# Pooled attention into a SiLU layer on one core: a prologue with gated dummies and value sums on TensorE

## The chip, the core and the metric

The kernel runs on one core of a Trainium2 chip. A core has five engines that run their own instruction streams and meet at semaphores: TensorE (PE, matrix products, whose weight loads are listed apart as PEld), VectorE (DVE), ScalarE (ACT, activation functions), GpSimd (POOL, which here mainly issues transfers) and SyncE (SP, transfers). Matrix products write into PSUM, eight banks of 128 partitions by 512 float32 values; the other tiles lie in SBUF. The metric is the time of one execution on the device in microseconds (us).

## What is computed

Attention over keys and values that are averaged in groups of eight tokens, then a layer with a SiLU between two matrix products. There are 8 batches, 8 heads, 576 tokens and 64 dimensions a head; the layer goes from 512 to 2048 and back to 512.

```python
def _attn_ref(q, k, v):                      # q, k, v: (8, 8, 576, 64)
    k_p = k.reshape(B, H, Sp, 8, D).mean(axis=3)          # Sp = 72
    v_p = v.reshape(B, H, Sp, 8, D).mean(axis=3)
    scores = np.matmul(q, k_p.transpose(0, 1, 3, 2)) / np.sqrt(D)
    attn = np.exp(scores - np.max(scores, axis=-1, keepdims=True))
    attn = attn / (np.sum(attn, axis=-1, keepdims=True) + 1e-09)
    return np.matmul(attn, v_p)

def _moe_ref(x, w_in, w_out):                # x: (4608, 512)
    h = x @ w_in                             # w_in: (512, 2048)
    return (h * (1.0 / (1.0 + np.exp(-h)))) @ w_out
```

## The kernel before

The kernel works on nine tiles of 512 tokens. While PE does the two products of tile t, the attention of the next batch is slipped in between its matmuls. For the first batch nothing can be hidden that way: its keys, queries and values must be loaded, pooled and multiplied before the first product can start. That stretch, some 20 us, is the prologue, and the change lies there.

The keys and values of a batch are 576 rows (8 heads by 72 groups) of 512 float32 values, eight tokens of 64 each. They are loaded as five "slots" of at most 128 rows, in two tiles: slots 0 to 2, and slots 3 and 4. `slot_sums` adds the eight tokens on DVE, in three halving steps:

```python
    def slot_sums(name, j, halves=False):
        raw = row_tiles[name][j]                       # j = 0: slots 0-2, j = 1: slots 3-4
        dst = rows5[name][:, SA:] if j else rows5[name][:, :SA]
        w = RE // 4 if halves else RE // 2             # RE = 512
        while w > D:                                   # D = 64
            nc.vector.tensor_add(out=raw[..., :w], in0=raw[..., :w], in1=raw[..., w : 2 * w])
            w //= 2
        nc.vector.tensor_add(out=dst, in0=raw[..., :D], in1=raw[..., D : 2 * D])
```

`select_k` and `select_v` bring the sums into the order that the attention needs, with matmuls against an identity matrix (`ident`) or its shifted columns (`shifts`); `copy_k` and `copy_v` take the results out of PSUM. `scores` multiplies keys with transposed queries and takes exponentials on ACT; `denominators` and `numerators` finish the softmax, and the numerators are multiplied into `xT`, the input of the first product:

```python
    def q_transpose(b, a, f):                          # a: heads 0-3 or 4-7, f: half of the tokens
        nc.vector.transpose(out=st["qT"][:, a, ...], in_=st["q_bf"][:, a, ...])

    def scores(b, segs):
        sc = [ps_tile([128, 512], FP32, "at", "sc_ps")[:SP, :w] for s in range(4)]
        for g, i0, i1, cs in seg_cols(segs):
            for c in range(2):
                for s in range(4):
                    nc.tensor.matmul(sc[s][:, cs], lhsT=kz..., rhs=st["qT"]..., start=(c == 0), stop=(c == 1))
        es = ...
        for s in range(4):
            nc.scalar.activation(es[:, s, :], sc[s], func=AF.Exp, scale=score_scale)

    def numerators(b, segs, tags=("at", "at")):        # (cut)
        for c in range(2):
            nu_ps = ps_tile([128, 512], FP32, tags[c], "nu_ps")
            ...                                        # four matmuls each, from vp and es
        for c in range(2):
            nc.vector.tensor_mul(out=xT[...], in0=nu[c]..., in1=rec...)
```

PSUM tiles come from two rings of banks, `banks = dict(mm=3, at=5)`: a new tile takes the bank of the one three (or five) before it and waits until that one has been read. `part(g, f)` is heads 4g to 4g+3 with half f of the tokens, written (g, f) in this text. The prologue itself:

```python
    def warm_up(n):                                    # dummies: keep TensorE's clock up
        for _ in range(n):
            nc.tensor.matmul(warm_ps, lhsT=warm[:, :128], rhs=warm, start=True, stop=True)

    ...                                                # loads of keys, queries, values
    nc.gpsimd.memset(shifts, 0.0)
    make_identity(nc, ident, nomemset=True)
    ...
    warm_up(19)
    slot_sums("k", 0)
    select_k(0, 0)
    copy_k(0, 0, act_copy)
    warm_up(4)
    q_transpose(0, 0, 0)
    scores(0, part(0, 0))
    slot_sums("k", 1)
    warm_up(3)
    select_k(0, 1)
    copy_k(0, 1, act_copy)
    q_transpose(0, 1, 0)
    warm_up(2)
    scores(0, part(1, 0))
    denominators(0, part(0, 0))
    slot_sums("v", 0)
    warm_up(2)
    select_v(0, 0, "mm")
    copy_v(0, 0, act_copy)
    denominators(0, part(1, 0))
    q_transpose(0, 0, 1)
    scores(0, part(0, 1))
    slot_sums("v", 1)
    warm_up(1)
    numerators(0, part(0, 0), ("mm", "at"))
    warm_up(2)
    select_v(0, 1, "mm")
    copy_v(0, 1)
    q_transpose(0, 1, 1)
    warm_up(2)
    numerators(0, part(1, 0), ("mm", "at"))
    scores(0, part(1, 1))
    warm_up(2)
```

Each line puts its instructions at the end of its engine's stream; every engine goes through its stream in order. After this the first product of tile 0 starts: for the first `GA` of 16 groups of hidden columns it does the first 288 tokens (`hp_ps`, then SiLU on ACT), then their other 224, and the rest of the groups with all 512 at once. The denominators and numerators of the second token halves, (0, 1) and (1, 1), are slipped in between.

Of the kernel before, what the change touches and what calls it, by code (L numbers as in the profile page):

```python
# [27 lines left out]
FP32 = mybir.dt.float32  # L28
# [8 lines left out]
def kernel(  # L37
# [9 lines left out]
    nc = tc.nc  # L47

    B, H, S, D = q.shape
    POOL = 8  # L50
    SP = S // POOL
# [30 lines left out]
    singles = ctx.enter_context(tc.tile_pool(name="singles", bufs=1))  # L82
# [8 lines left out]
    def ps_tile(shape, dtype, tag, name):  # L91
        return psum.tile(shape, dtype, tag=tag, bufs=banks[tag], name=name)
# [2 lines left out]

    shifts = singles.tile([128, SP + 128 + SP], BF16, name="shifts")
    ident = shifts[:, SP : SP + 128]
    ones = singles.tile([SP, 32], BF16, name="ones")
    warm = singles.tile([128, 512], BF16, name="warm")
    w_in_sb = singles.tile([128, KF, d_ff], BF16, name="w_in_sb")  # L100
# [49 lines left out]
    def q_transpose(b, a, f):  # L150
        st = batches[b]
        n = QF * D
        nc.vector.transpose(  # L153
            out=st["qT"][:, a, f * QF : (f + 1) * QF].rearrange("r i c p -> r (i c p)"),
            in_=st["q_bf"][:, a, f * n : (f + 1) * n],
        )
# [60 lines left out]
    def k_transpose(b, parts=(0, 1)):  # L217
        st = batches[b]
        kT_ps = ps_tile([128, 2, 2, SP], BF16, "at", "kT_ps")
        for a in parts:  # L220
            for c in range(2):
# [10 lines left out]
    RE = POOL * D  # L232
    ROWS = H * SP
    SLOTS = ROWS // 128
    REST = ROWS - 128 * SLOTS
    k5, v5 = (singles.tile([128, SLOTS + 1, D], BF16, name=f"{n}5") for n in "kv")
    rows5 = {"k": k5, "v": v5}


    SA = SLOTS - 1  # L240
    row_tiles = {
        n: [
            big.tile([128, m, RE], FP32, tag=f"{n}_raw2", name="raw") if i else
            raw_tile(f"{n}_raw", H, full=True)[:, : m * RE].rearrange(
                "r (i e) -> r i e", e=RE
            ) for i, m in enumerate((SA, SLOTS + 1 - SA))
        ] for n in "kv"
    }
# [20 lines left out]
    def slot_sums(name, j, halves=False):  # L269
        raw = row_tiles[name][j]  # L270
        dst = rows5[name][:, SA:] if j else rows5[name][:, :SA]
        w = RE // 4 if halves else RE // 2
        while w > D:
            nc.vector.tensor_add(  # L274
                out=raw[..., :w], in0=raw[..., :w], in1=raw[..., w : 2 * w]
            )
            w //= 2
        nc.vector.tensor_add(out=dst, in0=raw[..., :D], in1=raw[..., D : 2 * D])


    def segments(h):
        r = SP * h
        while r < SP * (h + 1):
            i = r // 128
            e = min(SP * (h + 1), 128 * (i + 1))
            yield i, (128 if i < SLOTS else REST), r - 128 * i, r - SP * h, e - r
            r = e

    def select_k(b, a):
        st = batches[b]  # L290
        if a == 0:
            st["kz_ps"] = ps_tile([128, 2, 2, SP], FP32, "at", "kz_ps")
        for c in range(2):
            for s in range(4):
                for i, n, r, sp, m in segments(4 * a + s):
                    nc.tensor.matmul(  # L296
                        st["kz_ps"][32 * s : 32 * (s + 1), a, c, sp : sp + m],
                        lhsT=k5[:n, i, c * DH : (c + 1) * DH],
                        rhs=ident[:n, r : r + m], start=True, stop=True,
                    )  # L300

    def copy_k(b, a, copy=nc.vector.tensor_copy):
        copy(out=kz[b % 2][:, a], in_=batches[b]["kz_ps"][:, a])
# [15 lines left out]
    def copy_v(b, a, copy=nc.vector.tensor_copy):  # L319
        hs = slice(4 * a, 4 * (a + 1))  # L320
        copy(out=batches[b]["vp"][:, hs, :], in_=batches[b]["v_ps"][:SP, hs, :])
# [3 lines left out]
    def part(g, f):  # L325
        return ((g, f * QF, (f + 1) * QF),)
# [6 lines left out]
    def width(segs):  # L333
        return QP * sum(i1 - i0 for _, i0, i1 in segs)
# [5 lines left out]
            yield g, i0, i1, slice(o, o + n)  # L340
            o += n

    def scores(b, segs):
        st = batches[b]
        w = width(segs)
        sc = [ps_tile([128, 512], FP32, "at", "sc_ps")[:SP, :w] for s in range(4)]
# [3 lines that stand above are left out]
                    rows = slice(32 * s, 32 * (s + 1))  # L350
                    nc.tensor.matmul(  # L351
                        sc[s][:, cs],
                        lhsT=kz[b % 2][rows, g, c, :],
                        rhs=st["qT"][rows, g, i0:i1, c, :],
                        start=(c == 0), stop=(c == 1),
                    )
        es = mid.tile([SP, 4, VW], BF16, tag="es", bufs=4, name="es")[:, :, :w]
        for s in range(4):
            nc.scalar.activation(es[:, s, :], sc[s], func=AF.Exp, scale=score_scale)  # L359
        st["es", segs] = es  # L360


    def denominators(b, segs, on_dve=False):
        st = batches[b]
        w = width(segs)
        es = st["es", segs]
        den_ps = ps_tile([128, 512], FP32, "at", "den_ps")
        for s in range(4):
            nc.tensor.matmul(  # L369
                den_ps[32 * s : 32 * (s + 1), :w],  # L370
                lhsT=ones, rhs=es[:, s, :], start=True, stop=True,
            )
        rec = mid.tile([128, VW], FP32, tag="rec", bufs=4, name="rec")[:, :w]
        if on_dve:
            nc.vector.reciprocal(rec, den_ps[:, :w])
        else:
            lnd = mid.tile([128, VW], FP32, tag="lnd", name="lnd")[:, :w]
            nc.scalar.activation(lnd, den_ps[:, :w], func=AF.Ln)  # L378
            nc.scalar.activation(rec, lnd, func=AF.Exp, scale=-1.0)
        st["rec", segs] = rec  # L380
# [318 lines left out]

    warm_ps = ps_tile([128, 512], FP32, "mm", "warm_ps")  # L700

    def warm_up(n):
        for _ in range(n):
            nc.tensor.matmul(warm_ps, lhsT=warm[:, :128], rhs=warm, start=True, stop=True)  # L704

    load_slots(nc.sync, 0, "k", 0, 2)
    load_slots(nc.scalar, 0, "k", 2, 3)
# [8 lines left out]
    attn_tables()  # L716
    nc.vector.memset(warm, 0.0)
    nc.vector.memset(ones, float(POOL))
    nc.gpsimd.memset(shifts, 0.0)
    make_identity(nc, ident, nomemset=True)  # L720

    for n in "kv":
        nc.vector.memset(row_tiles[n][1][REST:, SLOTS - SA], 0.0)
# [12 lines left out]
        load_w_in(512 * c, 512 * (c + 1))  # L736

    act_copy = nc.scalar.copy
    warm_up(19)
    slot_sums("k", 0)  # L740
    select_k(0, 0)
    copy_k(0, 0, act_copy)
    warm_up(4)
    q_transpose(0, 0, 0)
    scores(0, part(0, 0))
    slot_sums("k", 1)
    warm_up(3)
    select_k(0, 1)
    copy_k(0, 1, act_copy)
    q_transpose(0, 1, 0)  # L750
    warm_up(2)
    scores(0, part(1, 0))
    denominators(0, part(0, 0))
    slot_sums("v", 0)
    warm_up(2)
    select_v(0, 0, "mm")
    copy_v(0, 0, act_copy)
    denominators(0, part(1, 0))
    q_transpose(0, 0, 1)
    scores(0, part(0, 1))  # L760
    slot_sums("v", 1)
    warm_up(1)
    numerators(0, part(0, 0), ("mm", "at"))
    warm_up(2)
    select_v(0, 1, "mm")
    copy_v(0, 1)
    q_transpose(0, 1, 1)
    warm_up(2)
    numerators(0, part(1, 0), ("mm", "at"))
    scores(0, part(1, 1))  # L770
    warm_up(2)
    load_slots(nc.gpsimd, 1, "k", 0, 3)
    load_slots(nc.gpsimd, 1, "k", 3, 4)
    load_slots(nc.gpsimd, 1, "k", 4, 5)
# [14 lines left out]
    for t in range(NT):  # L789
        a = t + 1  # L790
        f_up, f_down = [], []
        if t == 0:
            GA = 11
            items = [(g, 0, HS) for g in range(GA)]
            items += [(g, HS, NTT - HS) for g in range(GA)]
            items += [(g, 0, NTT) for g in range(GA, KG)]
            f_up += [(1, lambda: denominators(0, part(0, 1), on_dve=True))]
            f_up += [(5, lambda: denominators(0, part(1, 1), on_dve=True))]
            f_up += [(13, lambda: numerators(0, part(0, 1)))]
            f_up += [(17, lambda: numerators(0, part(1, 1)))]  # L800
        else:
            G = lambda *gs: [(g, 0, NTT) for g in gs]
            if t == 1:
                items = (
                    G(12, 13, 14, 15) + [(0, "251")] + G(8) + [(0, "43")] + G(9)
                    + [(0, "7h6")] + G(10) + [(0, "s")] + G(11, 0, 1, 2, 3)
                )
            else:
                items = (
                    G(12, 13) + [(0, "251")] + G(14) + [(0, "43")] + G(15) + [(0, "76")]  # L810
                    + [(1, "2")] + [(0, "hs")] + [(1, "51")] + G(0) + [(1, "43")] + G(1)
                    + [(1, "7h6")] + G(2) + [(1, "s")] + G(3)
                )
            for n in U_X:
                f_up.append((0, lambda n=n: unit_x_sum(t, n)))
            for n in (2, 5):
                f_up.append((36 if t > 1 else 45, lambda n=n: hidden_sum(n, 4, 8)))
            f_up.append((56, lambda: hidden_sum(6, 4, 8)))
            for n, k0 in ((2, 0), (5, 0), (1, 4), (1, 0)):
                f_up.append((64, lambda n=n, k0=k0: hidden_sum(n, k0, k0 + 4)))  # L820
            f_down.append((33, lambda: hidden_sum(7, 0, 8)))
            f_down.append((71, lambda: hidden_sum(6, 0, 4)))
# [99 lines left out]
```

The softmax here doesn't subtract the row's maximum and nothing guards it: scores larger than these inputs give would overflow.

## Time and profile before

| what | value |
|---|---|
| time, median of 3 runs | 287.23 us (286.76 to 287.54) |
| span of the profiled execution | 284.8 us |
| granted TensorE clock | 1.000 |
| PE busy | 278.0 us (98%) |
| DVE busy | 225.1 us (79%) |
| ACT busy | 183.8 us (65%) |
| POOL busy | 52.2 us (18%) |
| first dummy matmul | 1.20 us |
| DVE begins the first key sums | 5.28 us |
| DVE begins the sums of the last value slots | 13.48 us |
| first SiLU | 20.04 us |

A profile is one execution as the hardware's profiler recorded it. A row of the timeline gives start and length in us, engine, line of the kernel, operation, output and inputs with their shapes, the number of instructions merged in it, and in brackets the idle time of the engine before it and what ended that. The chain that ended last is followed back from the last instruction, at each step to what released it. A line such as `L274` is that of the kernel before.

### The profile page before, as it was taken

To read this page: it belongs to the slowest core of one execution; us is meant where nothing else is said; L and a number is where in the kernel's file an instruction comes from. 1 tells how busy PE (TensorE), PEld (TensorE's weight loads), DVE (VectorE), ACT (ScalarE), POOL (GpSimd) and SP (SyncE) were. 2 spreads that over 40 slices of the span, in tenths; PEclk is the share of its full clock that TensorE was granted. 3 is DMA by queue.
4 is the path that set the end of the run, shared out by engine and by line. 5 is a ranking of instruction groups with operands and counts; after the bars stand their busy time and mean duration, and the time that the engine had idled before them with its cause. 6 is when DMAs were issued, how large, how long until landed. Compare 5 with 4: busy or idle time off the path is not lost.

```text
span 284.8 us, 6920 instructions
## 1 busy us (share of the span) xinstructions
PE 278.0 (98%) x2773; PEld 196.0 (69%) x2793; DVE 225.1 (79%) x403; ACT 183.8 (65%) x359; POOL 52.2 (18%) x68
## 2 busy tenths in 40 slices
PE   8989999999999999999999999999999999999995
PEld 3348544465777677767888886677677867787684
DVE  4887854979969796979698969986998686836773
ACT  1577676458656886688568857794779558325700
POOL 8664317402030011101200101054100000000000
PEclk9999999999999999999999999999999999999999
DMA  7999999793849565964895396839970032005004
GB/s 211 277 266 227 219 306 183 214 199 70 153 69 210 124 96 95 145 148 126 140 177 156 72 147 113 176 59 170 150 142 0 2 85 65 2 9 139 1 3 147
DMA packets 35296, 37.70 MB, mean 132 GB/s; under 512 B 9952, under 2 KB 27616, under 8 KB 35264
## 3 DMA queue, kind: packets, MB, share of 16 engines
q0 software_dynamic: 21760, 20.86, 43.0%
q1 hardware_dynamic: 12928, 15.48, 22.2%
q10 hardware_dynamic: 576, 0.92, 0.9%
q8 instruction: 22, 0.36, 0.6%
q14 instruction: 10, 0.08, 0.1%
HBM read 36.70 MB, written 9.44 MB: 162 GB/s over the span
## 4 chain that ended last, share of the span: by engine, by line
PE 94%; DVE 3%; ACT 1%; issue 1%; DVEq 0%
PE hp_ps L547 25%; PE o_psP L655 15%; PE o_psQ L655 15%; PE u_psQ L488 7%; PE u_psP L488 7%; PE o_psR L655 5%; PE sc_ps L351 4%; PE warm_ps L704 4%; PE o_ps L582 3%; PE nu_ps L395 3%; PE u_psR L488 2%; PE den_ps L369 2%; DVE w_sum L633 1%; PE kz_ps L296 1%; DVE xT L404 1%
## 5 line engine op out<-in xcount | busy, mean ns | idle before, releaser
L547 PE MATMUL hp_ps<-xT,w_in_sb 128*128 128x512 bf16 (+3 forms) x397 | 80.8, 338 | 1.4 <-ACT h_T L553 0.4
L655 PEld LDWEIGHTS <-h_sum 128*128 128x128 bf16 x640 | 60.6, 98 | 11.9 <-issue 1.3
L553 ACT ACTIVATE h_T<-hp_ps 128x512 bf16<-128x512 f32 (+2 forms) x95 | 51.4, 546 | 26.3 <-PE hp_ps L547 24.9
L547 PEld LDWEIGHTS <-w_in_sb 128*128 128x128 bf16 x412 | 39.3, 98 | 25.0 <-issue 1.4
L615 DVE TENSOR_TENSOR h_sum<-h_T 128x1024 bf16<-128x1024 bf16 (+1 forms) x72 | 50.8, 743 | 7.0 <-ACT h_T L553 7.0
L359 ACT ACTIVATE es<-sc_ps 72x384 bf16<-72x384 f32 (+1 forms) x100 | 39.0, 470 | 10.0 <-PE sc_ps L351 9.9
L488 PEld LDWEIGHTS <-w_sum 128*128 128x128 bf16 x300 | 29.4, 98 | 7.7
L655 PEld LDWEIGHTS <-h_T 128*128 128x128 bf16 x256 | 24.1, 98 | 4.4 <-issue 0.9
L404 DVE TENSOR_TENSOR xT<-nu_ps,rec 128x384 bf16<-128x384 f32 (+1 forms) x50 | 24.0, 532 | 0.3
L378 ACT ACTIVATE lnd<-den_ps 128x384 f32<-128x384 f32 (+1 forms) x23 | 11.1, 484 | 20.2 <-PE den_ps L369 20.2
L153 DVE STREAM_TRANSPOSE qT<-q_bf 128x576 bf16<-128x576 bf16 x32 | 23.0, 753 | 0.0
L182 POOL DMA_DIRECT2D raw<-in_k_dram x5 | 7.0, 1398 | 79.2 <-DVE h_sum L615 28.8
L496 ACT ACTIVATE h_T<-c_sb 128x512 bf16<-128x512 f32 x30 | 18.1, 625 | 5.0 <-DVE c_sb L520 5.0
L274 DVE TENSOR_TENSOR raw<-raw 128x384 f32<-128x384 f32 (+3 forms) x20 | 12.4, 618 | 7.5 <-DMA raw<-in_v_dram 4.3
L655 PE MATMUL o_psP<-w_out_sb,h_sum 128*128 128x256 bf16 x128 | 17.6, 273 | 0.0
L655 PE MATMUL o_psQ<-w_sum,h_sum 128*128 128x256 bf16 x128 | 16.7, 273 | 0.0
L655 PE MATMUL o_psQ<-w_out_sb,h_sum 128*128 128x256 bf16 x128 | 16.6, 273 | 0.0
L655 PE MATMUL o_psQ<-w_sum,h_T 128*128 128x256 bf16 x128 | 16.5, 273 | 0.0
L655 PE MATMUL o_psP<-w_sum,h_T 128*128 128x256 bf16 x128 | 16.5, 273 | 0.0
L520 DVE TENSOR_TENSOR c_sb<-u_psP,t_sb 128x512 f32<-128x512 f32 x15 | 10.2, 678 | 7.1 <-PE u_psP L488 3.6
L655 PE MATMUL o_psR<-w_sum,h_sum 128*128 128x256 bf16 x128 | 15.7, 273 | 0.0
L655 PE MATMUL o_psP<-w_sum,h_sum 128*128 128x256 bf16 x128 | 15.4, 272 | 0.0
(77 smaller groups left out, 417.1 us busy)
## 6 DMA issues: line engine op xcount, KB each, us to landing
out_dram<-o_sb SPq DMA_DIRECT2D x128, 64.0 KB, 3.0
q_bf<-in_q_dram POOLq DMA_DIRECT2D x6, 576.0 KB, 11.1
raw<-in_k_dram SPq DMA_DIRECT2D x6, 512.0 KB, 5.0
raw<-in_k_dram POOLq DMA_DIRECT2D x5, 576.0 KB, 9.1
raw<-in_v_dram POOLq DMA_DIRECT2D x5, 576.0 KB, 8.6
raw<-in_v_dram SPq DMA_DIRECT2D x5, 512.0 KB, 7.6
w_in_sb<-in_moe_w_in_dram POOLq DMA_DIRECT2D x8, 256.0 KB, 8.4
w_out_sb<-in_moe_w_out_dram POOLq DMA_DIRECT2D x4, 512.0 KB, 13.5
```

The costliest lines, as they stand in the source:

```text
L153: nc.vector.transpose(out=st["qT"][:, a, f * QF : (f + 1) * QF].rearrange("r i c p -> r (i c p)"), in_=st["q_bf"][:, a, f * n : (f + 1) * n],)
L274: nc.vector.tensor_add(out=raw[..., :w], in0=raw[..., :w], in1=raw[..., w : 2 * w])
L351: nc.tensor.matmul(sc[s][:, cs], lhsT=kz[b % 2][rows, g, c, :], rhs=st["qT"][rows, g, i0:i1, c, :], start=(c == 0), stop=(c == 1),)
L359: nc.scalar.activation(es[:, s, :], sc[s], func=AF.Exp, scale=score_scale)
L404: nc.vector.tensor_mul(out=xT[:, 2 * g0 + c : 2 * (g0 + ng - 1) + c + 1 : 2, cols], in0=nu[c][:, :w].rearrange("r (g n) -> r g n", g=ng), ...
L488: nc.tensor.matmul(ps[bank][:, u, :], lhsT=w[:, kk, 128 * u : 128 * (u + 1)], rhs=x[:, kk, :], start=first and u == 0 and kk == 0, stop=kk ...
L496: nc.scalar.activation(h_T[:, g : g + 2, j * NQ : (j + 1) * NQ], src, func=AF.Silu)
L547: nc.tensor.matmul(hp_ps[:, r0:r1], lhsT=w_in_sb[:, kk, g * 128 : (g + 1) * 128], rhs=xT[:, kk, x0 : x0 + r1 - r0], start=(kk == 0), stop= ...
L553: nc.scalar.activation(h_T[:, g, n0 : n0 + n], hp_ps[:, :n], func=AF.Silu)
L615: nc.vector.tensor_tensor(out=h_sum[n][:, ks, :], in0=quarter(*a, ks), in1=quarter(*b, ks), op=op)
L655: nc.tensor.matmul(ps[b][:, c, :], lhsT=left(n, kt, c), rhs=W_OUT[n][:, kt, :], start=b not in begun, stop=kt == k1 - 1, skip_group_check= ...
L704: nc.tensor.matmul(warm_ps, lhsT=warm[:, :128], rhs=warm, start=True, stop=True)
```

## The change

It has four parts.

Only nine dummies run freely at the start. Eight more, in float32 with 128 columns and zero weights, read the last columns of a loaded key slot, so they start once that slot is there. Those columns (384 to 511) are read by the sums but never written by them, so dummies and sums can run side by side.

The last two value slots are no longer summed on DVE: eight float32 matmuls with an identity matrix, one for each of the eight tokens of a group, add up in PSUM (`pool_slots`), and one copy on DVE (`copy_pooled`) rounds the sums to bfloat16. This needs the identity in float32 (`ident32`), from which ACT copies the bfloat16 one. Both value copies are now on DVE.

The two late query transpositions stand together, ahead of that copy; the second key half is summed and selected between the third and fourth exponential of the first scores; the numerators of (0, 0) come after the second value selection; some dummies go.

And `GA` is 12 for 11.

It is meant to take work off DVE in the stretch after the values have landed, and to let the dummies end when the key sums are there.

```diff
@@ -95,6 +95,8 @@
 
     shifts = singles.tile([128, SP + 128 + SP], BF16, name="shifts")
     ident = shifts[:, SP : SP + 128]
+    ident32 = singles.tile([128, 128], FP32, name="ident32")
+    warm32 = singles.tile([128, 128], FP32, name="warm32")
     ones = singles.tile([SP, 32], BF16, name="ones")
     warm = singles.tile([128, 512], BF16, name="warm")
     w_in_sb = singles.tile([128, KF, d_ff], BF16, name="w_in_sb")
@@ -277,6 +279,21 @@
             w //= 2
         nc.vector.tensor_add(out=dst, in0=raw[..., :D], in1=raw[..., D : 2 * D])
 
+
+    def pool_slots(name, p0, p1):
+        if p0 == 0:
+            pooled[name] = ps_tile([128, SLOTS + 1 - SA, D], FP32, "mm", "p_ps")
+        for p in range(p0, p1):
+            nc.tensor.matmul(
+                pooled[name], lhsT=ident32,
+                rhs=row_tiles[name][1][:, :, p * D : (p + 1) * D],
+                start=(p == 0), stop=(p == POOL - 1),
+            )
+
+    def copy_pooled(name):
+        nc.vector.tensor_copy(out=rows5[name][:, SA:], in_=pooled[name])
+
+    pooled = {}
 
     def segments(h):
         r = SP * h
@@ -340,7 +357,7 @@
             yield g, i0, i1, slice(o, o + n)
             o += n
 
-    def scores(b, segs):
+    def scores(b, segs, between=None):
         st = batches[b]
         w = width(segs)
         sc = [ps_tile([128, 512], FP32, "at", "sc_ps")[:SP, :w] for s in range(4)]
@@ -356,6 +373,8 @@
                     )
         es = mid.tile([SP, 4, VW], BF16, tag="es", bufs=4, name="es")[:, :, :w]
         for s in range(4):
+            if s == 3 and between:
+                between()
             nc.scalar.activation(es[:, s, :], sc[s], func=AF.Exp, scale=score_scale)
         st["es", segs] = es
 
@@ -699,9 +718,15 @@
 
     warm_ps = ps_tile([128, 512], FP32, "mm", "warm_ps")
 
-    def warm_up(n):
+    def warm_up(n, ps=warm_ps):
         for _ in range(n):
-            nc.tensor.matmul(warm_ps, lhsT=warm[:, :128], rhs=warm, start=True, stop=True)
+            nc.tensor.matmul(ps, lhsT=warm[:, :128], rhs=warm, start=True, stop=True)
+
+    def warm_behind(rhs, n):
+        for _ in range(n):
+            nc.tensor.matmul(
+                warm_ps[:, : rhs.shape[-1]], lhsT=warm32, rhs=rhs, start=True, stop=True
+            )
 
     load_slots(nc.sync, 0, "k", 0, 2)
     load_slots(nc.scalar, 0, "k", 2, 3)
@@ -716,8 +741,11 @@
     attn_tables()
     nc.vector.memset(warm, 0.0)
     nc.vector.memset(ones, float(POOL))
-    nc.gpsimd.memset(shifts, 0.0)
-    make_identity(nc, ident, nomemset=True)
+    nc.vector.memset(warm32, 0.0)
+    nc.vector.memset(ident32, 0.0)
+    nc.vector.memset(shifts[:, :SP], 0.0)
+    nc.vector.memset(shifts[:, SP + 128 :], 0.0)
+    make_identity(nc, ident32, nomemset=True)
 
     for n in "kv":
         nc.vector.memset(row_tiles[n][1][REST:, SLOTS - SA], 0.0)
@@ -736,39 +764,44 @@
         load_w_in(512 * c, 512 * (c + 1))
 
     act_copy = nc.scalar.copy
-    warm_up(19)
+    act_copy(ident, ident32)
+    warm_up(9)
+    warm_behind(row_tiles["k"][0][:, SA - 1, RE - 128 :], 8)
     slot_sums("k", 0)
     select_k(0, 0)
     copy_k(0, 0, act_copy)
     warm_up(4)
     q_transpose(0, 0, 0)
-    scores(0, part(0, 0))
-    slot_sums("k", 1)
-    warm_up(3)
-    select_k(0, 1)
-    copy_k(0, 1, act_copy)
+
+    def rest_k():
+        slot_sums("k", 1)
+        warm_up(3)
+        select_k(0, 1)
+        copy_k(0, 1, act_copy)
+
+    scores(0, part(0, 0), rest_k)
     q_transpose(0, 1, 0)
     warm_up(2)
     scores(0, part(1, 0))
     denominators(0, part(0, 0))
     slot_sums("v", 0)
-    warm_up(2)
+    pool_slots("v", 0, 3)
     select_v(0, 0, "mm")
-    copy_v(0, 0, act_copy)
+    pool_slots("v", 3, 5)
     denominators(0, part(1, 0))
+    pool_slots("v", 5, POOL)
     q_transpose(0, 0, 1)
+    q_transpose(0, 1, 1)
+    copy_pooled("v")
+    copy_v(0, 0)
     scores(0, part(0, 1))
-    slot_sums("v", 1)
     warm_up(1)
-    numerators(0, part(0, 0), ("mm", "at"))
-    warm_up(2)
     select_v(0, 1, "mm")
     copy_v(0, 1)
-    q_transpose(0, 1, 1)
-    warm_up(2)
+    numerators(0, part(0, 0), ("mm", "at"))
     numerators(0, part(1, 0), ("mm", "at"))
     scores(0, part(1, 1))
-    warm_up(2)
+    warm_up(2, ps_tile([128, 512], FP32, "mm", "warm_ps"))
     load_slots(nc.gpsimd, 1, "k", 0, 3)
     load_slots(nc.gpsimd, 1, "k", 3, 4)
     load_slots(nc.gpsimd, 1, "k", 4, 5)
@@ -790,7 +823,7 @@
         a = t + 1
         f_up, f_down = [], []
         if t == 0:
-            GA = 11
+            GA = 12
             items = [(g, 0, HS) for g in range(GA)]
             items += [(g, HS, NTT - HS) for g in range(GA)]
             items += [(g, 0, NTT) for g in range(GA, KG)]
```

## The prediction, made before the changed kernel had run

> **What bounds the kernel now.** I read the page's engine table first: TensorE (PE) is busy 98% of the 284.8 us span and the clock is granted in full, so time is only to be had where PE runs dummies or waits. Next the busy time by stretches, to find where that is.
>
> ```profile
> 8.00:13.48 5.48, 5.31 (x68) 2.33 (x69) 4.46 (x9) 3.46 (x12) 3.01 (x6) 1.00 1.14 280
> 13.48:17.57 4.09, 3.62 (x44) 1.49 (x46) 3.90 (x9) 2.77 (x9) 3.15 (x5) 1.00 1.24 207
> 17.57:20.50 2.93, 2.53 (x22) 1.31 (x21) 2.07 (x3) 2.90 (x7) 1.64 (x3) 1.00 1.18 287
> 20.50:28.40 7.90, 7.90 (x89) 6.07 (x88) 6.24 (x11) 6.13 (x17) 3.38 (x6) 1.00 1.14 248
> ```
>
> The columns after the length are PE, weight loads, DVE, ACT, POOL. From 20.5 us on PE has no idle time at all (7.90 of 7.90), and the stretches to 200 us are as full; before 20.5 much of its work is dummies. So the prologue is worth exactly what it moves the moment at which PE becomes full. In 13.48 to 17.57 DVE is the full one (3.90 of 4.09), in 17.57 to 20.50 ACT is (2.90 of 2.93). Third, the chain that ended last, for that moment:
>
> ```profile
> 15.80 0.42 DVE vp L321
> 16.23 0.69 DVE qT L153
> 16.92 0.04 issue
> 16.96 0.48 PE sc_ps L351 x8
> 17.44 1.29 ACT es L359 x4
> 18.73 0.02 issue
> 18.75 1.28 ACT L414
> 20.03 0.01 issue
> 20.04 0.42 ACT h_T L553
> 20.46 0.04 issue
> 20.50 0.40 PE hp_ps L547 x2
> ```
>
> The last query transposition on DVE releases the last scores, four exponentials and the load of the SiLU table follow on ACT, and the first SiLU at 20.04 frees the bank for which PE waits (PE may run three hp_ps groups ahead, three banks being there). I call that first SiLU S; S = 20.04. Fourth, DVE in order of time, for why the transposition comes so late:
>
> ```profile
> 12.09 0.77 DVE L153 STREAM_TRANSPOSE qT<-q_bf 128x576 bf16<-128x576 bf16 x1
> 13.48 1.15 DVE L274 TENSOR_TENSOR raw<-raw 128x512 f32<-128x512 f32 x2 [0.61 <-DMA raw<-in_v_dram]
> 14.66 0.29 DVE L278 TENSOR_TENSOR v<-raw 128x128 bf16<-128x128 f32 x1
> 14.87 0.81 DVE L404 TENSOR_TENSOR xT<-nu_ps,rec 128x288 bf16<-128x288 f32 x2
> 15.80 0.42 DVE L321 CAST vp<-v_ps 72x256 bf16<-72x256 f32 x1
> 16.15 0.76 DVE L153 STREAM_TRANSPOSE qT<-q_bf 128x576 bf16<-128x576 bf16 x1
> 16.84 0.78 DVE L404 TENSOR_TENSOR xT<-nu_ps,rec 128x288 bf16<-128x288 f32 x2
> ```
>
> DVE idles 0.61 us until the last value slots land at 13.48, then works without a gap to 17.62. Everything early is slack against that landing; what follows it sets S.
>
> [...] The kernel before has no float32 matmul, so no trace here shows it. [...] the dummies' weight loads are 0.43 us apart from 2.02 to 6.3 us, then six take 1.25 us, 0.21 each. [...] The trace shows no matmul overtaking another, and my argument rests on it: a matmul that waits for a DMA holds up all that stand behind it.
>
> **The change part by part.**
>
> *Gated dummies.* Now 19 dummies run from 1.20 to 8.04 while the first key sums end at 7.23: select_k starts about 0.7 us late. After: 9 x 0.43 from 1.20 end at 5.05, and 8 float32 ones start when a key slot has landed (5.28 or a little before). [...] About two at half clock and six at full: 2 x 0.43 + 6 x 0.26 = 2.4, end at 7.7. Gain at select_k 0.3 us. Sums of the second key tile end at 9.27 on DVE whatever PE does, so the second score group is ready perhaps 0.8 us earlier (its copy also moves ahead of the fourth exponential). None of this passes the landing at 13.48: worth 0.0 at S.
>
> *Identity.* Built in float32 on POOL after DVE memsets, and copied by ACT. POOL's affine select ended at 6.39, behind its own 0.38 us memset; the copy should end by about 6.5, before 7.2. Worth 0. POOL issues weights some 0.4 us sooner, but behind the values in its queue, so I keep the landing at 13.45.
>
> *Query transposition (1, f1)* goes from 16.15 into DVE's idle time before the landing (12.86 to 13.63). Takes 0.76 us off DVE after the landing.
>
> *Value sums on PE.* DVE loses 1.15 + 0.29 = 1.44 us and gains a copy of 128x128 from PSUM, about 0.28 (the 72x256 cast takes 0.42). PE gains eight float32 matmuls, c each. The first waits for both late value slots and stands in PE's order before select_v(0), the denominators of (1,0) and the scores of (0,1), which ran from 12.2 to 13.9 beside the transfer. They now run behind the landing.
>
> The chain after the landing, with T1 the end of the last pooling matmul: select_v 0.20 and denominators 0.35 (their steps in the chain of before) make T1 = 13.45 + 0.55 + 8c. Then on PE scores (0,1) 0.45 and a dummy 0.21. On DVE the pooled copy ends at T1 + 0.5 and the first value copy at T1 + 0.9; select_v(1) runs on PE to about T1 + 1.0, and its copy ends at T1 + 1.45. The first two multiplications, 0.81, end at T1 + 2.25. The scores of (1,1) need that: there are five "at" banks, and their fourth tile falls on the bank of the numerators (0,0), which DVE frees there (in PE's order after the change one of these score matmuls has exactly this DVE wait). First finished score tile at T1 + 2.65 as ACT sees it, exponentials 1.30, table load 1.28: S = T1 + 5.25 = 19.25 + 8c.
>
> With c = 0.213[...] S = 20.95, 0.9 later than 20.04. With c = 0.26, my choice, S = 21.33, 1.3 later. With c = 0.43[...] S = 22.7, 2.65 later. The break-even is c = 0.10[...].
>
> *Dummies removed.* Seven of 0.21 us in the middle; they lay in PE's waits. Worth 0.
>
> *GA 11 to 12.* One more hidden group split: four matmuls of 512 columns become four of 288 (55 take 6.14 us, 0.112 each) and four of 224 (about 0.10). 4 x (0.112 + 0.10 - 0.21) = about 0.01, at most 0.1 us on PE. On ACT 0.41 + 0.37 for 0.60.
>
> Sum: +1.3 + 0.05 = +1.35 us at full carry, since PE has no idle time behind S to absorb it. I take +1.2, 288.4 us, the small cut being for the rival below.
>
> **Rivals.** (a) The design works: DVE was the full engine after the landing, it loses 1.44 + 0.76 us there and gains 0.28, so S comes about 1 us earlier, 286.3. For it: DVE's 3.90 of 4.09, and a late transposition on the chain. Against it: PE takes over the sums serially with the blocked work, and all four multiplications plus two copies now stand behind the landing (before, one copy was ACT's and 0.81 us of multiplication filled a wait). This would also come out if the late slots landed a microsecond earlier than 13.4[...]: 0.1 or 0.2 us of this may appear through POOL's shorter work.
> (b) Float32 matmuls expose their weight loads: c near 0.43, eight gated dummies end after 8.5, pooling takes 3.4 us, and the result is +2.7, 289.9. For it: the sizes are small, 128 columns against 128 weight columns, and bf16 loads take 98 ns[...]. Against: eight dummies were evidently meant to cover 5.28 to 7.23, 0.24 each.
> (c) PE cools: it would idle from about 12 to 13.45 waiting for values; if the clock halves there, the next 3 us run at half speed, +0.5 to +1. Against: one gap of 1.5 us, with work on both sides.
> (d) Nothing moves: ACT or the hidden groups reabsorb it, 287.2. Against: PE is full from 20.5 on.
>
> **Range and chances.** Middle 288.4; (b) or (c) reach 289.8, (a) at a third of its strength reaches 286.8. I give (a) about one in five. Range 286.8 to 289.8. Two per cent is 5.7 us, more than the whole part of the prologue that could move: faster 0.005, within 0.985, slower 0.01.
>
> **What would show it.** Right: pooling matmuls start within 0.2 us of 13.45 after a PE wait on the value DMA, spaced 0.21 to 0.30; the first SiLU at 21.0 to 21.8; PE full from there; the first key selection near 7.5 with no effect later. In the last multiplications of the prologue, DVE ends near 19.2 against 17.62. Wrong: first SiLU before 20.0, a landing of the value slots before 12.7, a PE that reaches the pooling after the landing, or idle time of PE between 21 and 45 us that changes against before.

## The result, and the profile after

The changed kernel takes 288.69 us (median of six executions, 288.36 to 289.6) where the kernel before takes 286.97 us (median of six, the three behind the 287.23 us of the start among them): ratio 1.0066, 95% interval 1.0045 to 1.0087. It is slower by 1.7 us; 288.4 us was predicted. The size came out nearly as forecast, but two of the steps behind it did not hold.

The same four stretches in the changed kernel, with the columns PE, weight loads, DVE, ACT, POOL, then granted clock, DMA share and GB/s:

```profile
8.00:13.48 5.48, 3.89 (x42) 1.79 (x41) 5.04 (x9) 3.66 (x12) 3.63 (x6) 0.95 1.14 274
13.48:17.57 4.09, 4.08 (x34) 3.24 (x34) 0.35 (x2) 0.85 (x2) 2.72 (x5) 0.65 1.24 206
17.57:20.50 2.93, 2.40 (x33) 1.14 (x35) 2.15 (x6) 1.84 (x6) 1.47 (x2) 1.00 1.18 295
20.50:28.40 7.90, 7.58 (x74) 4.75 (x72) 7.25 (x10) 6.25 (x15) 3.62 (x6) 1.00 1.14 248
```

Between 13.48 and 17.57 PE and DVE have changed places: DVE falls from 3.90 us to 0.35, PE is full. In the stretch ahead of it PE is busy 3.89 us where it was 5.31. And the clock column has two numbers that no row of the kernel before had, 0.95 and 0.65.

The chain that ended last in the changed kernel, through the prologue (start, length, what):

```profile
4.83 7.98 DMA raw<-in_v_dram
12.81 0.14 issue
12.95 1.62 PE p_ps L287 x6
14.57 0.35 PE v_ps L331 x6
14.92 1.01 PE p_ps L287 x4
15.93 0.36 PE den_ps L388 x3
16.29 0.91 PE p_ps L287 x6
...
18.76 0.81 DVE xT L423 x2
19.57 0.04 issue
19.61 0.36 PE sc_ps L368 x5
19.97 1.28 ACT es L378 x4
21.25 0.02 issue
21.27 1.28 ACT L433
22.56 0.01 issue
22.57 0.42 ACT h_T L572
```

The transfer of the value slots now leads straight into the pooling products (p_ps; each float32 product is recorded as two matmuls, so x6 is three products), with select_v and the denominators between them as forecast, and the chain goes on through the multiplication into xT to the last scores, the exponentials and the table load. The first SiLU, S, is at 22.57 against 20.04. DVE in order of time shows how little is left there:

```profile
11.74 1.43 DVE L155 STREAM_TRANSPOSE qT<-q_bf 128x576 bf16<-128x576 bf16 x2
17.22 0.29 DVE L294 CAST v<-p_ps 128x128 bf16<-128x128 f32 x1 [4.05 <-PE p_ps L287]
```

The two transpositions are done before the landing, as meant; then DVE stands still for 4.05 us until the last pooling product. PE, DVE and ACT each keep to the order of their streams here. PE starts the value selection, whose sums DVE had ready at 11.83, at 14.57, behind three products. DVE takes out its result, which PE finished at 14.92, at 17.43, behind the cast that waited. And ACT starts the fourth exponential of the first scores, which PE finished at 9.05, at 10.58, behind the copy of the second key selection, for which ACT waited 0.33 us.

This profile is one of the two executions out of six (289.6 and 289.3 us) whose mean clock was 0.994 and 0.993; the other four, at 1.000, lie between 288.36 and 288.86 us. To see the change without that, both kernels were profiled again (below, with the experiments). The chain of the changed kernel in its second profile, at full clock throughout, which I call the undisturbed one:

```profile
12.99 0.91 PE p_ps L287 x6
13.90 0.20 PE v_ps L331 x6
14.11 0.53 PE p_ps L287 x4
14.63 0.24 PE den_ps L388 x4
14.87 0.86 PE p_ps L287 x6
15.73 0.37 PE sc_ps L368 x8
...
19.82 1.28 ACT L433
21.11 0.01 issue
21.12 0.42 ACT h_T L572
```

The same steps from the same landing: the pooling pieces take 0.91 + 0.53 + 0.86 = 2.30 us instead of 1.62 + 1.01 + 0.91 = 3.54, and S is 21.12, not 22.57.

### The profile page after: what moved, and what is told of

The parts are those of the page before. It is cut to its first block, busy times and chain, and to the rows that moved or that the text cites. A ratio compares the mean times of both kernels' runs of the same rounds, so it can differ in the third digit from the quotient of the medians.

```text
span 287.7 us, 6964 instructions
## 1 busy us (share of the span) xinstructions
PE 279.1 (97%) x2794; PEld 200.0 (69%) x2813; DVE 224.4 (78%) x406; ACT 184.2 (64%) x360; POOL 52.2 (18%) x67
## 4 chain that ended last, share of the span: by engine, by line
PE 88%; DMA 4%; DVE 3%; issue 1%; POOL 1%; ACT 1%; SPq 0%; DVEq 0%; POOLq 0%
PE hp_ps L566 24%; PE o_psP L674 15%; PE o_psQ L674 14%; PE u_psQ L507 7%; PE u_psP L507 7%; PE o_psR L674 5%; PE sc_ps L368 4%; PE o_ps L601 3%; DMA raw<-in_v_dram 3%; PE nu_ps L414 2%; PE u_psR L507 2%; PE den_ps L388 2%; PE p_ps L287 1%; DVE xT L423 1%; DVE w_sum L652 1%
## 5 line engine op out<-in xcount | busy, mean ns | idle before, releaser
L601 PE MATMUL o_ps<-w_out_sb,h_T 128*128 128x512 bf16 x61 | 14.5, 380 | 0.3 <-issue 0.3
```

The lines of the kernel that those rows point to most:

```text
L601: nc.tensor.matmul(ps, lhsT=h_T[:, g, m * 128 : (m + 1) * 128], rhs=w_out_sb[:, g, :], start=(g == 0), stop=(g == KG - 1),)
```

## The experiments

After the comparison the theory was: in-order work held up behind the landing, plus eight float32 products, plus in some executions a halved clock that follows PE's idle time. The rivals: that the products alone are at fault, that the clock alone is, or that one of the small parts (the gated dummies, the regrouped hidden columns) costs something. S below is from the profile of each kernel. The ratio is against the kernel before on the same chip; it is the recorded one, which differs a little from the quotient of the two medians.

| run | S, us | median, us | before, us | ratio, 95% interval |
|---|---|---|---|---|
| changed kernel | 22.57 | 288.69 | 286.97 | 1.0066 (1.0045 to 1.0087) |
| e1 gap filled | 21.18 | 288.47 | 286.67 | 1.0057 (1.0037 to 1.0076) |
| e2 pooling later | 20.31 | 287.79 | 286.67 | 1.0037 (1.0024 to 1.0051) |
| e3 sums on DVE | 19.50 | 288.34 | 286.67 | 1.0054 (1.0029 to 1.0079) |
| e8 the same, four dummies more | 19.60 | 286.95 | 287.16 | 0.9995 (0.9982 to 1.0008) |
| e7 GA 11 | 22.62 | 289.39 | 286.67 | 1.0081 (1.0051 to 1.0110) |
| e4 gate alone | 19.38 | 287.21 | 287.16 | 1.0008 (0.9994 to 1.0023) |
| e5 early transposition alone | 19.24 | 286.78 | 287.16 | 0.9988 (0.9976 to 1.0000) |
| e6 and early scores | 18.77 | 286.39 | 287.16 | 0.9970 (0.9956 to 0.9984) |
| e12 e6 with the gate | 18.34 | 285.91 | 286.93 | 0.9971 (0.9956 to 0.9986) |

### Six dummies in PE's gap

The edit, on the changed kernel:

```diff
     slot_sums("v", 0)
+    warm_up(6)
     pool_slots("v", 0, 3)
```

> The changed kernel with six more free dummies (6 x 0.21 us) on PE just before the pooling, where its trace shows PE idle for 1.43 us and the clock at half for the 3.4 us that follow. Theory order (the loss is the work that PE holds back behind the wait for the values[...]; the half clock is an extra that only two of the six timed executions showed): clock 1.00 in every execution, pooling products 0.24 to 0.28 us each instead of 0.44, first SiLU near 21.1 us instead of 22.57, median 288.3 us, none above 288.8. Rival clock (the half clock is the whole loss): 287.0 us.

PE's idle time ahead of the first pooling product falls from 1.43 to 0.26 us:

```profile
13.06 0.91 PE L287 MATMUL p_ps<-raw,ident 128*128 128x128 f32 x6 [0.26 <-DMA raw<-in_v_dram]
```

All seven executions ran at a clock of 0.998 to 1.000. The first SiLU comes at 21.18, and from the landing at 13.06 that is 8.12 us, the same as the 8.13 of the undisturbed profile (12.99 to 21.12; a landing is taken here and below as the start of the first instruction that waited for it); the profile with half the clock has 9.62. So the 1.45 us between the two profiles of the changed kernel are the clock, and a held clock leaves nearly the whole loss standing: ratio 1.0057, with one execution (288.95 us) above the 288.8 that was to be the most. The clock is an addition, not the cause of the main loss.

### The pooling behind the scores

The eight products move behind the first scores of the second half, so that select_v(0), the denominators and those scores can run during the transfer:

```diff
     slot_sums("v", 0)
-    pool_slots("v", 0, 3)
+    warm_up(2)
     select_v(0, 0, "mm")
-    pool_slots("v", 3, 5)
     denominators(0, part(1, 0))
-    pool_slots("v", 5, POOL)
     q_transpose(0, 0, 1)
     q_transpose(0, 1, 1)
-    copy_pooled("v")
     copy_v(0, 0)
     scores(0, part(0, 1))
     warm_up(1)
+    pool_slots("v", 0, POOL)
+    copy_pooled("v")
     select_v(0, 1, "mm")
```

> The changed kernel with all eight pooling products behind the scores of (0,1) in PE's order, and the copy of the first values ahead of the pooled copy on DVE: nothing but the second value selection now waits for the late values. Theory order: the first value selection, the denominators (1,0) and the scores (0,1) run before the landing again, first SiLU 20.2 to 20.6 us, time 287.0 to 287.5 us. Rival products (float32 products are slow by themselves, 0.44 us each even without a drop of the clock): first SiLU 21.5, 288.4 us.

The chain that ended last, in this kernel:

```profile
13.22 0.32 PE warm_ps L723
13.54 1.80 PE p_ps L287 x16
15.34 0.02 issue
15.36 0.30 DVE v L294
```

Ahead of the products stands PE's own work, no longer the transfer, and eight products in one piece take 1.80 us: 0.225 us each. S falls from 21.18 to 20.31 against the first experiment, the ratio from 1.0057 to 1.0037, some 0.6 us. The two ran on the same chip, and by the means of their 7 and 13 executions the difference is 0.58 us, with a 95% interval of about 0.2 to 0.9. That is what the blocked order costs. Of the loss, the other two thirds remain, so the time misses the 287.0 to 287.5 us that the theory gave.

### The last value slots summed on DVE again

The order of PE is that of the second experiment, without the products; the gate, the transpositions, the multiplications and the hidden groups stay as changed. The second edit adds four dummies to the first:

```diff
     copy_v(0, 0)
+    slot_sums("v", 1)                    # in place of all pool_slots and copy_pooled
     scores(0, part(0, 1))
-    warm_up(1)
+    warm_up(5)                           # e8 only
     select_v(0, 1, "mm")
```

> The changed kernel with the last value slots summed on DVE again (no pooling products), everything else kept: gated dummies, both late query transpositions ahead of the sums, numerators (0,0) behind the second value selection. Theory order: first SiLU 19.7 to 20.1, time 286.7 to 287.1 us, that is the time before: the whole loss lies in the pooling on PE. Rival arrangement (the loss lies in the numerators and copies that now stand behind the landing): 287.8 us or more.

> The run with the last value sums on DVE (no pooling products) and four more dummies behind the scores of (0,1), where its trace shows PE idle for 0.89 us and the clock at half from 16.3 to 19.8 us. Theory order, amended by that run (there the dummies left out cost as much as the pooling did): clock 1.00 in all executions, first SiLU 19.4 to 19.7 us, time 286.3 to 286.8 us, that is 0 to 0.5 us under before. Rival arrangement: 287.5 us or more with the clock held too.

The first of the two stays at 1.0054: by its time alone the rival, the arrangement, would have been right. But seven of its eight executions had a clock of 0.986 to 0.994, and the only one at 0.998 took 286.77 us. In its profile S is early, 19.50, and yet the time is close to that of the changed kernel. Its stretches around the loss:

```profile
14.00:15.00 1.00, 0.11 (x4) 0.10 (x2) 0.78 (x3) 1.00 (x4) 1.00 (x3) 1.00 1.24 205
17.00:18.00 1.00, 1.00 (x4) 0.32 (x3) 0.22 (x1) 1.00 (x4) 0.11 (x1) 0.50 1.24 202
19.00:20.00 1.00, 1.00 (x8) 0.32 (x6) 1.00 (x1) 0.90 (x2) 0.45 (x2) 0.50 1.14 350
```

PE stands idle for 0.89 us between 14 and 15, waiting for the sums, and from 16.8 to 20.2 each stretch has half the clock. Four dummies in that wait (e8) leave S where it was, 19.60, hold the clock at 0.998 or more in all 14 executions, and bring the ratio to 0.9995. So the arrangement is not the loss. The step from 1.0054 to 0.9995 is 1.7 us for four dummies of 0.21 us.

With the clock held in both, e2 against e8 is the price of the float32 products alone: 1.0037 against 0.9995, 1.2 us. The two ran on different chips, each beside the kernel before, and with both intervals the difference lies between some 0.7 and 1.7 us; at S it is 0.71.

### When the clock halves

Three profiles have the half clock. Where it began and ended is read from short stretches; below are the busy times of that interval and, above it, of one of equal length before it. Changed kernel, then e7, then e3:

```profile
9.48:12.90 3.42, 2.04 (x28) 0.77 (x26) 3.35 (x6) 2.77 (x10) 2.18 (x4) 1.00 1.16 257
12.90:16.31 3.41, 3.36 (x21) 2.89 (x21) 0.27 (x1) 0.44 (x1) 2.58 (x4) 0.50 1.24 205
```

```profile
10.16:13.58 3.42, 2.29 (x31) 1.30 (x29) 3.00 (x5) 2.74 (x9) 2.51 (x4) 1.00 1.16 257
13.58:16.99 3.41, 3.41 (x23) 2.91 (x21) 0.00 (x0) 0.97 (x3) 2.67 (x5) 0.50 1.25 207
```

```profile
13.39:16.80 3.41, 2.31 (x39) 1.00 (x31) 2.85 (x9) 2.19 (x7) 2.95 (x5) 1.00 1.24 206
16.80:20.21 3.41, 3.41 (x22) 1.17 (x18) 1.81 (x3) 2.99 (x6) 1.45 (x3) 0.50 1.21 262
```

Each time the clock is halved for 3.41 us, though PE is full, and each time PE was busy only 2.04 to 2.31 us (60 to 68%) in the 3.41 us before. The longest single gaps were 1.43, 1.13 and 0.89 us. The length of the gap alone does not order the cases, for the undisturbed profile has a gap of 1.06 us and no halving. There the 3.41 us that hold the gap, 10.20 to 13.62, have PE busy for 2.36 us, or 69%. All other stretches of that length, measured end to end through the prologues, were 84% busy or more, and none of them was followed by half a clock. So the busy share orders the cases, but 68% with a halving and 69% without one lie too close together to name a limit, and what decides it was not shown.

The halvings also began close to multiples of 3.41 us after the clock's rise at the start. When that rise came is an estimate from the gated dummies. Eight take 2.02 us where the clock is up already (e4, and the same in e1) and 2.49 in the changed kernel. At half speed half of the time is lost, so 0.47 us lost are 0.94 us at half speed, and the clock rose near 5.01 + 0.94 = 5.95, twice 3.41 and 0.1 us before 12.90. In e7 the same reckoning (2.82 us) gives 6.6, twice 3.41 us before 13.58 to within 0.15, and in e3 (2.76 us) 6.5, three times 3.41 us before 16.80 to within 0.1. Whether that is more than chance, three profiles do not show.

One such halving is 3.41 x 0.5 / 287.7 = 0.6% of the clock's mean. By this estimate an execution at 0.994 had one and one at 0.988 two; a profile with two was not taken.

### GA back to 11

```diff
-            GA = 12
+            GA = 11
```

> The changed kernel with GA = 11. Theory order: within 0.1 us of the changed kernel, 288.6 us. Rival split (the twelfth split hidden group costs PE small products and ACT one more SiLU on the path): 288.3 us or less.

Inconclusive. Five of the eight executions had a clock of 0.988 to 0.994; the three at full clock (287.76, 288.35, 288.77 us) have a mean 0.25 us below that of the four of the changed kernel (288.36 to 288.86), which so few executions do not resolve. The execution that took longest (292.9 us) is left out of the ratio. A difference of less than half a microsecond stays open.

### The gate alone

The kernel before with nine dummies, eight gated ones and the float32 identity, nothing else (new tiles, helper and memsets cut):

```diff
-    warm_up(19)
+    act_copy(ident, ident32)
+    warm_up(9)
+    warm_behind(row_tiles["k"][0][:, SA - 1, RE - 128 :], 8)
```

> The kernel before with the gated dummies alone (9 free ones, 8 float32 ones behind the key slot, identity built in float32 and copied by ACT; values, transpositions and everything later as before). Theory order: first key selection 0.3 to 0.7 us earlier, first SiLU 19.9 to 20.2 us as before, time within 0.3 us of the kernel before. Rival key landing (the gating itself costs time later): slower by 0.8 us or more. Side question, the wait of DVE for key sums near 143 us that every profile of the changed family shows (0.3 to 1.0 us) and that of the kernel before does not: if it comes with the two added 128x128 float32 tiles it shows here and in the dummies run, and not in the other two.

No difference in time: 1.0008, 0.9994 to 1.0023. Yet its first SiLU is at 19.38, earlier than the 19.9 to 20.2 expected and than 20.04 in the profile of before. How far S of one kernel varies had to be known. As to the side question: the wait for key sums does not come with the added tiles, for it is also in e5 (1.2 us) and e6 (1.4 us), which lack them.

### Both kernels again

> The kernel before, unchanged, looked at once more. Question: DVE waits for key sums between 110 and 150 us in every profile since the first one (0.3 to 1.4 us), also in kernels that lack the added tiles. Theory (the margin of those loads is thin in the kernel before too, and varies from one execution to the next): a wait of 0.3 us or more shows here as well. Rival (the changed prologue brings it by shifting the transfers): none here. The landing of the late values: 12.6 to 13.5 us, first SiLU 6.6 to 6.8 us after it.

> As the look before it, a second one, for the spread: theory and rival the same.

> The changed kernel, unchanged, looked at once more, since its first profile had the clock at half for 3.4 us. With the clock held: pooling products near 0.24 to 0.28 us each, first SiLU 7.9 to 8.2 us after the landing of the values (9.6 with the half clock).

PE in order of time, the first key selection, in the first, second and third profile of before:

```profile
7.97 0.28 PE L296 MATMUL kz_ps<-shifts,k 128*32 128x72 bf16 x12
```

```profile
8.26 0.28 PE L296 MATMUL kz_ps<-shifts,k 128*32 128x72 bf16 x12
```

```profile
7.30 0.28 PE L296 MATMUL kz_ps<-shifts,k 128*32 128x72 bf16 x12 [0.22 <-DVE k L278]
```

S is 20.04, 20.33 and 19.37: 12.07 us after the first key selection in all three, and 12.08 in the gated kernel (7.30, 19.38). From the landing of the last value slots (13.48, 12.80, 12.85) it is 6.56, 7.53 and 6.52, not the 6.6 to 6.8 expected. So in the kernel before S is tied to PE's front, not to the landing. The chain that ended last says the same in the first profile already, in the part ahead of the lines shown with the prediction:

```profile
1.20 6.84 PE warm_ps L704 x19
8.04 0.21 PE kz_ps L296 x8
...
15.38 0.33 PE v_ps L314 x6
```

It goes back through PE's work to the first dummies, and no transfer of values stands in it.

The 19 dummies end sooner or later as the clock rises early or late, and all of PE's work behind them moves along: their weight loads close up at 4.54, 6.29 and 7.09 us in the third, first and second profile, and the selection starts at 7.30, 7.97 and 8.26. In the third it waits 0.22 us for the sums, which end at 7.25, so there a still earlier rise would not have started it before 7.3.

In the changed kernel it is the reverse: S is 8.1 us after the landing at full clock whether the first key selection is at 7.31 (e1) or 7.85 (e11). In that profile the changed kernel took 287.57 us, and three executions of before on the same chip 286.86, 286.19 and 286.66. The wait for key sums that the theory expected in the kernel before as well, 0.3 us or more, was not there: none in the second profile, 0.2 us in the third.

### The early transposition, and the last scores ahead of the numerators

Both on the kernel before. The first edit is only the move of the late transposition; the second also moves the last scores:

```diff
     q_transpose(0, 0, 1)
+    q_transpose(0, 1, 1)
     scores(0, part(0, 1))
     ...
     copy_v(0, 1)
-    q_transpose(0, 1, 1)
-    warm_up(2)                               # e6, e12
-    numerators(0, part(1, 0), ("mm", "at"))  # e6, e12
     scores(0, part(1, 1))
+    numerators(0, part(1, 0), ("mm", "at"))  # e6, e12
```

> The kernel before with the last query transposition alone moved ahead of the last value sums, into DVE's idle time before the landing. Theory order: scores (1,1) 0.4 to 0.5 us earlier, first SiLU 19.5 to 19.7 us, time 0.3 to 0.5 us shorter than before. Rival (the transposition is not what the chain needs): within 0.1 us of before.

> As the early transposition, and the scores of (1,1) ahead of the numerators (1,0) in PE's order, so that the last four exponentials follow the four before them on ACT (all dummies but two kept). Theory order: exponentials (1,1) from 16.3 us, first SiLU 18.8 to 19.1 us, time 0.8 to 1.2 us shorter than before. Rival (the multiplications of (1,0) on DVE at 17.6 to 17.9 us bound the first product as much as ACT does): first SiLU 19.5 or later, 0.3 us.

> The kernel before with two parts together: the gated dummies, and the early transposition with the scores of (1,1) ahead of the numerators (1,0). First key selection near 7.3 us in place of 7.3 to 8.3, first SiLU 18.2 to 18.5 us. Theory give-back (an earlier start reaches the loads of later keys sooner, and DVE waits for them between 110 and 190 us): the waits of DVE for key sums add up to 1 us or more and the time is 0.6 to 1.2 us shorter than before, about that of the early scores alone. Rival (the gain at the first SiLU is carried to the end): 1.5 us shorter than before or more.

The early transposition by itself is worth something: 0.9988 (0.9976 to 1.0000), about 0.35 us. At S it is as much: 19.24 is 11.75 us after that kernel's first key selection (7.49), 0.32 less than 12.07. With the last scores ahead of the numerators it is 0.9970, about 0.86 us, and this kernel beats both the one before and the changed one. ACT in order of time in e6 shows why:

```profile
14.77 2.69 ACT L359 ACTIVATE es<-sc_ps 72x288 bf16<-72x288 f32 x8
17.48 1.28 ACT L414 ACT_TABLE_LOAD   x1
18.77 1.01 ACT L553 ACTIVATE h_T<-hp_ps 128x288 bf16<-128x288 f32 x3
```

All eight exponentials stand in one row and the table load follows at once. In the kernel before it began at 18.75.

The gate added to this (e12) moves S to 18.34 and leaves the ratio where it was, 0.9971. An earlier S is not kept to the end. The loads of ACT's function tables are good marks to follow that, since each kernel has them at the same places in its work; their starts, in us:

| kernel | S | first SiLU table | near 141 | near 156 | near 251 |
|---|---|---|---|---|---|
| before | 20.04 | 18.75 | 141.95 | 156.81 | 251.46 |
| before, third profile | 19.37 | 18.07 | 141.28 | 156.07 | 250.96 |
| e4 gate alone | 19.38 | 18.08 | 141.29 | 156.64 | 251.49 |
| e12 | 18.34 | 17.04 | 140.24 | 156.19 | 250.79 |
| changed, first profile | 22.57 | 21.27 | 144.49 | 159.82 | 254.42 |
| changed, undisturbed profile | 21.12 | 19.82 | 143.04 | 157.83 | 252.43 |

e12 is 1.71 us ahead of the kernel before up to the third mark and 0.62 at the fourth; e4 is 0.66 ahead and then 0.17. The waits of e12 between 60 and 200 us have the reason (who waited for what: total, times, longest):

```profile
DVE raw L190 <- DMA raw<-in_k_dram: 1.1, 1, 1.1
```

DVE waits 1.1 us for the keys of a later batch to land; it is 0.8 in e4, 1.4 in e6, 0.2 in the third profile of before and nothing in the other two. Most kernels that come to that point early find the transfer late. It does not go strictly by S: the third profile of before has the S of e4 and keeps most of its lead, and e2, with S at 20.31, waits 1.0 us all the same. What sets the landing of those keys was not tried, and stays open.

## Why the prediction came out as it did

**PE is full behind S, so S is carried: right.** The first profiles differ by 2.53 us at S, 2.52 at the first table load and 2.54 at the one near 144, and by 2.9 in the span. The undisturbed profile is 1.07 us behind the first profile of before at the first load, 1.09 near 143 and 0.97 near 252. Nothing absorbed it on the way. The opposite does not hold: in e12 more than half of a lead, 1.1 of 1.7 us, was lost at the keys.

**Value sums on PE: right, in mechanism and size.** The pooling starts on the transfer (12.95, after 1.43 us of idle PE), select_v, denominators and scores stand behind it, and with c = 0.26 my S was 7.88 us after the landing. It is 8.13. That c was my estimate, for the kernel before has no float32 product to measure. The last pooling product ends 2.74 us after the landing (I had 0.55 + 8 x 0.26 = 2.63), S comes 5.39 us later (I had 5.25; the terms add up to 5.23). c was 0.225 us in one piece (e2), 0.29 in the three pieces of the undisturbed profile. On PE alone the trade costs 1.2 us (e2 against e8) and the blocked order 0.6 (e1 against e2).

**"Everything early is slack against that landing": wrong.** I took the end of one DVE wait at 13.48 for the point from which S is counted. The kernel before counts from its first key selection, 12.07 us in three profiles, and the landing itself moves between 12.8 and 13.48. In the profile that I had, both were close together: DVE had worked off what followed the landing at 15.68, and the value selection on PE that released the next copy ended at 15.71. But the chain of that profile ran through PE, and I read it only from 15.80 on. In the changed kernel, where S does count from the landing, what is early is slack indeed. The mistake did little harm to the sum: S of before averages 19.91 over three profiles, so the change at full clock is 21.12 - 19.91 = +1.2 us where I had 21.33 - 20.04 = +1.29.

**The landing kept at 13.45: off by 0.5 us**, 12.95 to 13.06 in the changed kernel and 12.80 and 12.85 in the later profiles of before. It is not the change that moved it, so rival (a) does not gain by it. The pooling did not start within 0.2 us of 13.45, then; of the other signs, S lay in the range of 21.0 to 21.8 in the undisturbed profile and outside it, at 22.57, in the first.

**"Dummies removed, worth 0": wrong.** Rival (c) said that PE would cool in the wait; I had it down for 0.5 to 1 us and argued against it that there was one gap of 1.5 us, with work on both sides. A gap of 1.43 us with work on both sides was enough. It happened in two of six executions, for 1.45 us at S and about 1 us in time (289.3 and 289.6 against 288.475, the median of the four at full clock). It also raised the median by about 0.2 us over that of those four. Six dummies went from the middle, not the seven that I counted. They were doing work that no busy column shows: e3 lost 1.7 us for the lack of four.

**Rival (b)**, a product near 0.43 us because its weight loads are exposed, was not the mechanism: at full clock a product is 0.225. The 3.54 us of pooling that it forecast (3.4) appear in the first profile, from the halved clock. On that profile alone (b) would have looked right.

**Query transposition: forecast as a relief, and it is one**, about 0.35 us alone (e5), which in the changed kernel is outweighed by the pooling. **Gate: 0** in time as I said, for another reason: in its one profile S is 0.5 us ahead of the mean of before, and none of that is left in the time. **GA** at 0.01 to 0.1 us was not resolved.

The sum then: +1.5 us at full clock (288.475 against 286.97) where I had +1.35 and took +1.2, and +0.2 by the clock. S accounts for 1.2 of the 1.5; the other 0.3 is no more than the spread of the four executions. That the forecast of 288.4 lies within 0.3 us of the result is in part luck: the forecast of the difference, +1.2, was 0.5 short of the +1.7 measured, and the median of the kernel before fell by 0.26 us when three more executions were added to those I started from.

## What to carry to other kernels

Before work moves into an engine's stream, write down what stands behind it: here the first pooling product waited 1.43 us for its transfer, and the value selection, denominators and scores, which had run beside the transfer, came after it, for 0.6 us of a 1.7 us loss. Dummies in a wait are not to be counted by their own time alone: here four of 0.21 us, or 0.84 us, made a difference of 1.7 us, and the 3.41 us that hold the wait had PE busy for 85% with them (e8, 12.22 to 15.63) and for 68% without (e3). And before calling something slack, follow the chain that ended last back to its start, and profile the same kernel two or three times: here the distance from the first key selection to S was the same in all of them, and that from the landing was not.

## What was not expected of the hardware

Gaps of 0.89 to 1.43 us were followed by half a clock on TensorE, for 3.41 us each time and in some executions of the same program only; a gap of 1.06 us in the undisturbed profile was not. The clock's rise at the start also came at different times in kernels whose first dummies are alike: the dummies' weight loads close up from 0.43 to 0.21 us at about 4.5, 6.3 and 7.1 us in three profiles of the kernel before, all beginning at 1.2. The first closed-up weight loads in the third, first and second profile:

```profile
4.54 2.04 PEld L704 LDWEIGHTS <-warm 128*128 128x128 bf16 x10 [0.23 <-issue]
6.29 1.25 PEld L704 LDWEIGHTS <-warm 128*128 128x128 bf16 x6 [0.28 <-issue]
7.09 0.75 PEld L704 LDWEIGHTS <-warm 128*128 128x128 bf16 x4 [0.22 <-issue]
```

S differs by up to a microsecond between these profiles, and PE's front with it. The record of the granted clock says 1.00 there, from the first dummy on, in all three, so the rise is inferred from the spacing of the weight loads, which halves. A float32 product of 128 by 128 by 128 takes 0.225 us back to back in e2, about as long as a bfloat16 dummy with 512 columns, 0.21 us; with the start-up of the first one counted in, these eight take 1.95 us and the eight gated dummies of e4 2.02 us, 0.24 and 0.25 each. It was 0.44 on average where most of the pooling ran at half the clock (3.54 / 8).
